# Expert weights subtracted on VectorE alone, x transposed through two PSUM banks, and the last chunk's second tile three units behind the first

## The chip, the cores and the metric

The kernel runs on one core of a Trainium2 chip. The metric is the device time of one execution in microseconds (us). The engines are named as the profile names them: PE is TensorE's matmuls and PEld its weight loads, DVE is VectorE, ACT is ScalarE, POOL is GpSimd, SP is SyncE, which issues most DMAs.

## What is computed

Three layers follow each other. All inputs are float32.

```python
# attention with a threshold: 4 batches, 8 heads, 576 positions, 64 per head
scores = scale * q @ k.T;  keep scores >= max - tau;  softmax;  @ v
x = attn_out.transpose(0, 2, 1, 3).reshape(2304, 512)
# top-1 mixture of 8 experts, D = 512, F = 1024
e_idx = argmax(x @ w_gate)
for e in range(8):
    mask = e_idx == e
    h = maximum(x[mask] @ w1[e], 0)
    out[mask] = gate_w[mask] * eom[mask, e] * (h @ w2[e])
# dense layer, 512 -> 2048 -> 512
h = x @ w_in;  g = maximum(0.01 * h, h);  return g @ w_out
```

## The kernel before

A float32 operand of a matmul is split in two parts that TensorE takes at its faster rate (fp32r): a "hi" part, which a cast makes, and a "lo" part, which is the operand less its hi part. Each product is the sum of three matmuls (`PASSES`): hi by hi, hi by lo, lo by hi. So each block of weights and each block of x needs a cast (L1554 on ACT, L1556 on DVE) and a subtraction (L1559, on DVE or POOL).

The program has an attention stage, an expert stage and a dense stage. In the expert stage there is one window of tokens for each place r = 0 to 7, in order of size (`CAPS` = 400, 368, 324, 320, 296, 272, 248, 216 columns), after a first window of 216. A window's work is:

- eight weight blocks (q = 0 to 7, 128x1024 each) loaded by SP into a ring of four buffers `raw` (`r_raw`), cast (`hi`) and subtracted (`lo`) into a ring of 12 in `arena` (`r_w`). The buffer in `raw` comes free when the subtraction has ended;
- three or four tiles of at most 108 tokens, fetched by a gather that POOL issues (L1627), transposed by TensorE into a PSUM bank (L1636, "xT"), cast (`xh`) and subtracted (`xl`) out of that bank into `arena`. The ring `r_tp` has as many places as transposed tiles may hold a bank;
- the first product, eight groups of 12 matmuls (L1667, "L1"), each into a bank of its own, at most three at a time (`r_l1`); its result goes through a ReLU on ACT (`hh`, L1675) and a subtraction on DVE (`hl`, L1681), which frees the bank;
- the second product, eight groups of 12 matmuls (L1708, "L2") into four banks.

PSUM has eight banks, which all of this shares. Meanwhile DVE also cuts the 64-bit words of the dense layer's weights down to float32 (`narrow`, four operations to a block: L1304, L1310, L1316, L1326).

The dense stage takes chunks of 512 tokens, and a last one of 256 (n = 256, two tiles of 128). A chunk has 16 units f. A unit is 12 matmuls of the first product (L1870, "h2"), then on ACT and DVE the leaky ReLU (`t`, L1877, and `g`, L1881) and the split of g (`gh`, L1554; `gl`, L1559), then for each tile three matmuls of the second product (L1896, "out") into the tile's bank. After the last unit each tile is scaled out of PSUM by ACT (L1919, "oev") and scattered to the result by an indirect DMA that POOL issues (L1925, "st").

No order is written out by hand. `Plan` holds a list of operations, each with its candidate engines and their costs, its dependencies, the rings it takes from (`acq`) and gives back to (`rel`), and a priority, which is a due time. It places them one after the other at the earliest time on an engine, and emits them in order of the planned start; on the chip each engine then runs its own list strictly in that order, and waits where data or a buffer is not there.

Of the kernel before, what the change touches and what calls it, by code (L numbers as in the profile page):

```python
# [8 lines left out]
F32 = mybir.dt.float32  # L9
# [1519 lines left out]
def experts(pl, ctx, tc, st, R, ar, w1, w2, w_in, w_out, xrows, yT, wtab, wf, out):  # L1529

    nc = tc.nc
    ps, bk, ident = st.ps, st.bk, st.ident
# [4 lines left out]
    r_raw, r_w, r_x, r_h, r_sm, r_ys = Ring(len(raw)), Ring(ar.NW), Ring(ar.NX), Ring(ar.NH), Ring(len(sm)), Ring(len(ys))  # L1537
    r_l1, r_tp, r_l2 = Ring(3), Ring(1), Ring(1)
    AD = ("act", "dve")
# [6 lines left out]
    def ev(n, ptr=0.0):  # L1546
        return (0.16 + 0.00083 * n + ptr, 0.14 + 0.00106 * n + ptr)
# [4 lines left out]
    def copy(o, out, in_):  # L1552
        if o.eng == "act":
            nc.scalar.copy(out=out, in_=in_)  # L1554
        else:
            nc.vector.tensor_copy(out=out, in_=in_)  # L1556

    def subtract(o, out, in0, in1):
        (nc.vector if o.eng == "dve" else nc.gpsimd).tensor_tensor(out=out, in0=in0, in1=in1, op=ALU.subtract)  # L1559


    free = st.t_over + 0.1


    wins, t = [(None, PRE, 0.0)], 96 * mm(PRE) + 4
# [8 lines left out]
    for r, n, tw in wins:  # L1574
# [7 lines left out]
        for q in range(4 if r is None else 0, 8):  # L1582
# [13 lines left out]
            if r is None and q < 6:  # L1596
                t = staged(st, q)
# [12 lines left out]
            O["lo", r, q] = pl.add(  # L1610
                *((("dve", "pool"), (1.5, 2.7)) if r is not None else ("dve", 1.4)), lambda o, f=lo, ld=ld, h=a: f(o, ld, h), [a], need - 11.9, rel=[(r_raw, ld)], label="lo", at=free + 3 if r is None else free)

# [212 lines left out]
    chunks = [(c, min(512, NT - c)) for c in range(0, NT, 512)]  # L1825
    r_o, r_g, r_t, r_h2 = Ring(1), Ring(2), Ring(2), Ring(4)
    tgs = [ys_ for ys_ in st.tg]
# [4 lines left out]
    for ci, (c0, n) in enumerate(chunks):  # L1832
# [24 lines left out]
        AHEAD = 8  # L1857
        outs = None
        for f in range(FF // 128):
# [22 lines left out]

            def g_hi(o, tt, n=n):
                copy(o, ar.g(o.slots[r_g][0])[:, 0, 0:n], tgs[tt.slots[r_t][0]][:, 1, 0:n])

            def g_lo(o, tt, gh, n=n):
                t = ar.g(gh.slots[r_g][0])
                subtract(o, t[:, 1, 0:n], tgs[tt.slots[r_t][0]][:, 1, 0:n], t[:, 0, 0:n].bitcast(F32))

            def prod(o, first, gh, f=f, u=u, c2=c2, m=m):  # L1890
                w = V[u, 1].rearrange("p a (c f) -> p a c f", c=2)
                g = ar.g(gh.slots[r_g][0])
                k = 0
                for gi, wi in ((0, 0), (0, 1), (1, 0)):
                    for t in range(m):
                        nc.tensor.matmul(  # L1896
                            out=bank(first, t), lhsT=g[:, gi, 128 * t:128 * t + 128], rhs=w[:, wi, c2, :],
                            start=(f == 0 and k == 0), stop=(f == FF // 128 - 1 and k == 2),
                        )
                    k += 1  # L1900
# [4 lines left out]
            gg = pl.add("dve", ev(n)[1], lambda o, a=a, tt=tt, f=act_g: f(o, a, tt), [tt], bf + 3.1, rel=[(bk, a), (r_h2, a)], label="g")  # L1905
            gh = pl.add(AD, (0.62, 0.4), lambda o, tt=tt, f=g_hi: f(o, tt), [gg], bf + 3.2, acq=[(r_g, 1)], label="gh")
            gl = pl.add("dve", 0.74, lambda o, tt=tt, gh=gh, f=g_lo: f(o, tt, gh), [gh], bf + 3.3, rel=[(r_t, tt)], label="gl")
            last_o = pl.add(
# [5 lines left out]
        for t in range(m):  # L1914
# [8 lines left out]
            def st_o(o, e, t=t, c0=c0):  # L1923
# [5 lines left out]

            e = pl.add(AD, ev(512, 0.1), lambda o, fb=outs, f=oev: f(o, fb), [last_o, e, mts[c0 // 128 + t]], base + CH + t, acq=[(r_sm, 1)],  # L1930
                       rel=[(bk, outs), (r_o, outs)] if t == m - 1 else [], label="oev")
# [132 lines left out]
```

## Time and profile before

| | |
|---|---|
| median of 3 runs | 1006.02 us (1003.82 to 1007.94) |
| the profiled execution | 1004.9 us, of which the span from first to last instruction is 1002.7 us |
| PE busy | 960.8 us, 96% of the span |
| DVE busy | 641.3 us, 64% |
| ACT busy | 507.3 us, 51% |
| POOL busy | 264.4 us, 26% |
| expert stage | about 338 to 595 us of the span |
| dense stage | about 595 us to the end |

A share of busy time over the whole span is a mean over the stages. The granted clock of TensorE is 1.00 at 2.4 GHz and 0.50 at 1.2 GHz.

### The profile page before, as it was taken

What the parts mean: (1) busy time and instruction counts of PE and PEld (TensorE: products, weight loads), DVE (VectorE), ACT (ScalarE), POOL (GpSimd) and SP (SyncE); (2) the same over time, 40 slices, a digit from 0 to 9 for tenths busy, and PEclk for the clock granted to TensorE, in tenths of its full rate; (3) what the DMA queues carried; (4) which work ended last, traced back from release to release, by engine and by line L of the source; (5) the groups of instructions that cost most, each with busy time, mean ns of one, the idle gap of its engine ahead of it and who ended that gap; (6) DMA issues with size and microseconds to landing.
All of it is one profiled execution on the core that took longest, in us unless ns stands there. A gap on an engine that the chain in (4) does not pass through costs nothing. (4 is left out here: it accounts for less than half of the span.)

```text
span 1002.7 us, 16909 instructions
## 1 busy us (share of the span) xinstructions
PE 960.8 (96%) x6118; PEld 844.5 (84%) x6118; DVE 641.3 (64%) x1231; ACT 507.3 (51%) x1009; POOL 264.4 (26%) x325
## 2 busy tenths in 40 slices
PE   6999999999999889999899999999999999999994
PEld 6788888888887789989899998888888888888883
DVE  7888998998996775988986548983223223222331
ACT  7778787888874355454555435443223222322321
POOL 4433333333112444442446402321000100100000
PEclk9999999999999899999999999999999999999998
DMA  5523432431242688589887552422000200100000
GB/s 143 150 71 90 129 72 74 138 81 49 75 152 69 191 222 293 190 303 305 301 286 266 166 178 77 119 70 74 11 1 1 84 1 0 63 1 1 18 25 22
DMA packets 63578, 114.32 MB, mean 114 GB/s; under 512 B 15424, under 2 KB 32832, under 8 KB 62976
## 3 DMA queue, kind: packets, MB, share of 16 engines
q1 hardware_dynamic: 56912, 92.02, 29.4%
q0 software_dynamic: 6576, 21.15, 7.6%
q8 instruction: 50, 0.82, 0.3%
q14 instruction: 40, 0.33, 0.1%
HBM read 84.72 MB, written 19.09 MB: 104 GB/s over the span
## 5 line engine op out<-in xcount | busy, mean ns | idle before, releaser
L1870 PE MATMUL ps<-arena 128*128 128x512 f32 (+1 forms) x960 | 207.6, 368 | 0.0
L1896 PE MATMUL ps<-arena 128*128 128x512 f32 x864 | 206.8, 389 | 0.0
L1870 PEld LDWEIGHTS ps<-arena 128*128 128x128 f32 x960 | 168.7, 188 | 30.9
L1559 DVE TENSOR_TENSOR arena<-raw,arena 128x512 fp32r<-128x512 f32 (+2 forms) x131 | 122.7, 941 | 111.1 <-PE ps L1896 67.0
L1896 PEld LDWEIGHTS ps<-arena 128*128 128x128 f32 x864 | 161.3, 188 | 33.2 <-ACT arena L1554 0.2
L1554 ACT CAST arena<-raw 128x1024 fp32r<-128x1024 f32 (+2 forms) x153 | 121.4, 803 | 107.5 <-PE ps L1896 56.4
L1881 DVE TENSOR_TENSOR raw<-ps,raw 128x512 f32<-128x512 f32 (+1 forms) x80 | 50.6, 636 | 134.3 <-ACT raw L1877 134.2
L1708 PE MATMUL ps<-arena 128*128 128x216 f32 (+7 forms) x864 | 128.9, 307 | 6.4 <-ACT arena L1675 4.7
L1708 PEld LDWEIGHTS ps<-arena 128*128 128x128 f32 x864 | 122.7, 193 | 7.4 <-ACT arena L1675 5.1
L1667 PE MATMUL ps<-arena 128*128 128x400 f32 (+7 forms) x768 | 114.1, 308 | 8.7 <-ACT arena L1554 3.2
L493 DVE SCALAR_TENSOR_TENSOR em<-ps,th,e 128x576 f32<-128x576 f32 x144 | 115.6, 811 | 9.2 <-ACT e L485 8.4
L1877 ACT ACTIVATE raw<-ps 128x512 f32<-128x512 f32 (+1 forms) x80 | 43.9, 553 | 150.9 <-PE ps L1870 150.9
L1667 PEld LDWEIGHTS ps<-arena 128*128 128x128 f32 x768 | 110.9, 190 | 10.3 <-DVE arena L1559 3.7
L474 DVE TENSOR_REDUCE nm<-ps 128x1 f32<-128x576 f32 x144 | 107.3, 752 | 17.0 <-PE ps L465 15.2
L485 ACT ACTIVATE e<-ps,nm 128x576 f32<-128x576 f32 x144 | 105.9, 744 | 6.8 <-DVE nm L474 6.2
L465 PE MATMUL ps<-k,qt 128*128 128x288 f32 x512 | 99.5, 322 | 2.3 <-ACT qt L256 0.9
L1925 POOL DMA_INDIRECT out_dram<-sm,oidx x18 | 17.8, 987 | 302.7 <-ACT sm L1919 269.8
L250 ACT COPY eta<-ps 128x512 f32<-128x512 f32 (+1 forms) x152 | 79.4, 543 | 23.3 <-PE ps L522 19.9
L522 PE MATMUL ps<-ident,em 128*128 128x128 f32 x576 | 84.2, 274 | 2.1 <-DVE em L493 1.3
L465 PEld LDWEIGHTS ps<-k,qt 128*128 128x128 f32 x512 | 74.6, 193 | 8.2 <-DVE em L493 2.5
L1559 POOL TENSOR_TENSOR arena<-raw,arena 128x1024 fp32r<-128x1024 f32 x23 | 58.8, 2562 | 61.7 <-ACT arena L1554 59.9
L601 PE MATMUL ps<-eta,rv 128*64 128x288 f32 x512 | 69.5, 412 | 1.9 <-ACT eta L250 1.9
(221 smaller groups left out, 1087.7 us busy)
## 6 DMA issues: line engine op xcount, KB each, us to landing
raw<-in_moe_w_dram SPq DMA_DIRECT2D x70, 512.0 KB
k<-k POOLq DMA_DIRECT2D x30, 304.0 KB
dw<-in_moe_w_in_dram SPq DMA_DIRECT2D x16, 512.0 KB
dw<-in_moe_w_out_dram SPq DMA_DIRECT2D x16, 512.0 KB
rk<-in_k_dram SPq DMA_DIRECT2D x16, 256.0 KB
rq<-in_q_dram SPq DMA_DIRECT2D x16, 256.0 KB
rv<-in_v_dram SPq DMA_DIRECT2D x16, 256.0 KB
xrows<-xt SPq DMA_DIRECT2D x4, 1024.0 KB
```

Source lines behind the costliest of these rows:

```text
L250: nc.scalar.copy(out=out, in_=in_)
L465: nc.tensor.matmul(out=s[:, c, :], lhsT=lhs, rhs=T[kk, P][:, off + c * HALF:off + (c + 1) * HALF], start=(m == 0), stop=(m == 2 * len(ops) ...
L474: nc.vector.tensor_reduce(out=T["nm", n], in_=T["sc", n], axis=AX.XY, op=ALU.max, negate=True)
L485: nc.scalar.activation(out=T["e", n].rearrange("p (a c) -> p a c", a=2), in_=T["sc", n], func=AF.Exp, bias=T["nm", n][:, 0:1], scale=1.0,)
L493: nc.vector.scalar_tensor_tensor(out=T["em", P, t][:, h, :].rearrange("p (a c) -> p a c", a=2), in0=T["sc", n], scalar=T["th", n][:, 0:1], ...
L522: nc.tensor.transpose(out=bank(o)[:, c * 128:(c + 1) * 128], in_=T["em", P, t][:, h, 64 * h + c * 128:64 * h + (c + 1) * 128], identity=ident,
L1554: nc.scalar.copy(out=out, in_=in_)
L1559: (nc.vector if o.eng == "dve" else nc.gpsimd).tensor_tensor(out=out, in0=in0, in1=in1, op=ALU.subtract)
L1667: nc.tensor.matmul(out=bank(o)[:, 0:n], lhsT=w[:, wi, 128 * f:128 * f + 128], rhs=xx[:, xi, c, :], start=(c == 0 and i == 0), stop=(c == K ...
L1708: nc.tensor.matmul(out=bank(first, d)[:, 0:n], lhsT=w[:, wi, k0:k0 + 128], rhs=hx[:, xi, :], start=(f == 0 and i == 0), stop=(f == 7 and i ...
L1870: nc.tensor.matmul(out=bank(o)[:, 0:n], lhsT=w[:, wi, c, 128 * c2:128 * c2 + 128], rhs=y[:, c, 0:n], start=(k == 0), stop=(k == 3 * KD - 1),)
L1896: nc.tensor.matmul(out=bank(first, t), lhsT=g[:, gi, 128 * t:128 * t + 128], rhs=w[:, wi, c2, :], start=(f == 0 and k == 0), stop=(f == FF ...
```

## The change

Three edits in `experts`. The places of `r_tp` go from one to two. The subtraction of an expert's weights has DVE as its only candidate, planned at 1.25, where it had DVE at 1.5 or POOL at 2.7. In the chunk with two tiles, each unit's products are two operations, one for each tile, and the second tile's has a due time three units later; the split of g there goes to a ring of four half-width buffers (`r_gs`) in the two buffers that `r_g` had, with smaller planned costs, and the first tile is scaled out as soon as its own products are done.

```diff
-    r_l1, r_tp, r_l2 = Ring(3), Ring(1), Ring(1)
+    r_l1, r_tp, r_l2 = Ring(3), Ring(2), Ring(1)
...
             O["lo", r, q] = pl.add(
-                *((("dve", "pool"), (1.5, 2.7)) if r is not None else ("dve", 1.4)), lambda o, f=lo, ld=ld, h=a: f(o, ld, h), [a], need - 11.9, rel=[(r_raw, ld)], label="lo", at=free + 3 if r is None else free)
+                "dve", 1.25 if r is not None else 1.4, lambda o, f=lo, ld=ld, h=a: f(o, ld, h), [a], need - 11.9, rel=[(r_raw, ld)], label="lo", at=free + 3 if r is None else free)
...
-    r_o, r_g, r_t, r_h2 = Ring(1), Ring(2), Ring(2), Ring(4)
+    r_o, r_g, r_t, r_h2, r_gs = Ring(1), Ring(2), Ring(2), Ring(4), Ring(4)
+
+    BEHIND = 3
...
-        outs = None
+        outs, before, tiles = None, last_o, [None] * m
...
+            def g_at(o, n=n):
+                if n > 256:
+                    return ar.g(o.slots[r_g][0])[:, :, 0:n]
+                i = o.slots[r_gs][0]
+                return ar.g(i // 2)[:, :, 256 * (i % 2):256 * (i % 2) + n]
...
-            gh = pl.add(AD, (0.62, 0.4), lambda o, tt=tt, f=g_hi: f(o, tt), [gg], bf + 3.2, acq=[(r_g, 1)], label="gh")
-            gl = pl.add("dve", 0.74, lambda o, tt=tt, gh=gh, f=g_lo: f(o, tt, gh), [gh], bf + 3.3, rel=[(r_t, tt)], label="gl")
+            small = m == 2
+            gh = pl.add(AD, (0.36, 0.3) if small else (0.62, 0.4), lambda o, tt=tt, f=g_hi: f(o, tt), [gg, before if small else None], bf + 3.2,
+                        acq=[(r_gs if small else r_g, 1)], label="gh")
+            gl = pl.add("dve", 0.45 if small else 0.74, lambda o, tt=tt, gh=gh, f=g_lo: f(o, tt, gh), [gh], bf + 3.3, rel=[(r_t, tt)], label="gl")
+            if small:
+                for t in range(2):
+                    o = pl.add(
+                        "pe", 3 * 0.228, lambda o, gh=gh, f=prod, fb=outs, t=t: f(o, fb or o, gh, ts=(t,)), [gl, *wo, tiles[t], outs],
+                        bf + 5.4 + 5.4 * BEHIND * t, acq=[(bk, 2), (r_o, 1)] if outs is None else [], rel=[(r_gs, gh)] if t else [], label="out")
+                    outs = outs or o
+                    tiles[t] = last_o = o
+                continue
...
-            e = pl.add(AD, ev(512, 0.1), lambda o, fb=outs, f=oev: f(o, fb), [last_o, e, mts[c0 // 128 + t]], base + CH + t, acq=[(r_sm, 1)],
+            e = pl.add(AD, ev(512, 0.1), lambda o, fb=outs, f=oev: f(o, fb), [tiles[t] or last_o, e, mts[c0 // 128 + t]], base + CH + t, acq=[(r_sm, 1)],
```

The planner turns these into other orders on each engine from the expert stage on. TensorE's list at the start of the expert stage, where L1708 with 216 columns is the first window's second product, L1636 are the transposes of x and L1667 with 400 columns is the first product of the window r = 0. Before:

```order
L1708 MATMUL ps<-arena 128x216 x12
L1636 MATMUL ps<-ident,sm_70 128x108 x4
L1708 MATMUL ps<-arena 128x216 x36
L1636 MATMUL ps<-ident,sm_71 128x108 x4
L1708 MATMUL ps<-arena 128x216 x36
L1636 MATMUL ps<-ident,sm_72 128x108 x4
L1708 MATMUL ps<-arena 128x216 x12
L1636 MATMUL ps<-ident,sm_73 128x76 x4
L1667 MATMUL ps<-arena 128x400 x96
```

The same place of the change:

```order
L1708 MATMUL ps<-arena 128x216 x12
L1636 MATMUL ps<-ident,sm_70 128x108 x4
L1708 MATMUL ps<-arena 128x216 x12
L1636 MATMUL ps<-ident,sm_71 128x108 x4
L1708 MATMUL ps<-arena 128x216 x24
L1636 MATMUL ps<-ident,sm_72 128x108 x4
L1636 MATMUL ps<-ident,sm_73 128x76 x4
L1708 MATMUL ps<-arena 128x216 x48
L1636 MATMUL ps<-ident,sm_70 128x108 x4
L1636 MATMUL ps<-ident,sm_71 128x108 x4
L1667 MATMUL ps<-arena 128x400 x96
```

The last tile of r = 0 (128x76) stood right ahead of L1667 and now stands 48 matmuls ahead of it, and the first two tiles of r = 1 have come in between. TensorE's list two windows on, where L1708 with 368 columns is the second product of r = 1 and L1667 with 324 columns the first product of r = 2, as a difference:

```order
 L1667 MATMUL ps<-arena 128x368 x96
 L1708 MATMUL ps<-arena 128x368 x12
 L1636 MATMUL ps<-ident,sm_70 128x108 x4
-L1708 MATMUL ps<-arena 128x368 x36
+L1708 MATMUL ps<-arena 128x368 x12
 L1636 MATMUL ps<-ident,sm_71 128x108 x4
-L1708 MATMUL ps<-arena 128x368 x24
+L1708 MATMUL ps<-arena 128x368 x12
 L1636 MATMUL ps<-ident,sm_72 128x108 x4
-L1708 MATMUL ps<-arena 128x368 x24
+L1708 MATMUL ps<-arena 128x368 x60
 L1667 MATMUL ps<-arena 128x324 x96
```

The last transpose stood 24 matmuls ahead of L1667 and now stands 60 ahead. TensorE's last rows, where L1870 (L1872 in the changed file) is h2 and L1896 (L1904) is out; before, and then of the change:

```order
L1870 MATMUL ps<-arena 128x256 x12
L1896 MATMUL ps<-arena 128x512 x6
L1870 MATMUL ps<-arena 128x256 x12
L1896 MATMUL ps<-arena 128x512 x18
L2059 UNCONDITIONAL_BRANCH
```

```order
L1872 MATMUL ps<-arena 128x256 x12
L1904 MATMUL ps<-arena 128x512 x6
L1872 MATMUL ps<-arena 128x256 x12
L1904 MATMUL ps<-arena 128x512 x27
L2077 UNCONDITIONAL_BRANCH
```

Nine products more stand behind the last h2. By the PSUM banks that the built program writes, the 27 alternate between the tiles in groups of three, second tile first, until the first tile has its last group, and the nine at the very end are all the second tile's; before, every group of six served both tiles.

## Rows read from the trace of the kernel before

**Rows 1.** The page, its first part: busy time, share of the span, instructions

```profile
PE 960.8 (96%) x6118; PEld 844.5 (84%) x6118; DVE 641.3 (64%) x1231; ACT 507.3 (51%) x1009; POOL 264.4 (26%) x325
```

**Rows 2.** Busy time by stretch: stretch, length, PE, PEld, DVE, ACT, POOL, clock, DMA share, GB/s

```profile
380.00:600.00 220.00, 212.55 (x1548) 209.20 (x1547) 164.21 (x222) 106.98 (x185) 90.81 (x57) 1.00 0.76 253
410.00:530.00 120.00, 114.07 (x806) 112.41 (x805) 107.53 (x133) 62.66 (x104) 51.21 (x28) 1.00 0.84 284
354.80:358.00 3.20, 0.49 (x2) 0.23 (x2) 3.03 (x9) 2.54 (x5) 2.82 (x2) 1.00 0.87 278
358.00:364.00 6.00, 6.00 (x25) 5.95 (x26) 5.64 (x6) 2.24 (x5) 2.49 (x2) 0.72 1.00 322
595.00:988.90 393.90, 393.89 (x1829) 329.45 (x1828) 160.81 (x240) 126.33 (x226) 37.52 (x31) 1.00 0.12 39
```

**Rows 3.** Waits in 330 to 600 us: us in total, times, longest

```profile
ACT arena L1554 <- DMA raw<-in_moe_w_dram: 19.4, 12, 5.3
```

**Rows 4.** Timeline of PE, expert stage: start, us, instruction, [idle before <-releaser]

```profile
356.21 0.45 PE L1667 MATMUL ps<-arena 128*128 128x400 f32 x1 [1.44 <-ACT arena L1554]
357.96 4.32 PE L1667 MATMUL ps<-arena 128*128 128x400 f32 x15 [1.29 <-DVE arena L1559]
...
431.34 0.41 PE L1667 MATMUL ps<-arena 128*128 128x324 f32 x1 [1.73 <-ACT arena L1554]
432.22 4.99 PE L1667 MATMUL ps<-arena 128*128 128x324 f32 x32 [0.46 <-DVE arena L1559]
...
492.42 3.40 PE L1667 MATMUL ps<-arena 128*128 128x296 f32 x23 [1.17 <-DVE arena L1559]
...
499.81 6.87 PE L1667 MATMUL ps<-arena 128*128 128x296 f32 x48 [1.75 <-DVE arena L1681]
...
528.44 1.78 PE L1667 MATMUL ps<-arena 128*128 128x272 f32 x12 [0.81 <-DVE arena L1681]
```

**Rows 5.** Groups by form, DVE and POOL, 380 to 600 us: busy us, mean ns

```profile
L1559 DVE TENSOR_TENSOR arena<-raw,arena 128x1024 fp32r<-128x1024 f32 x41 | 53.6, 1322 | 22.3 <-ACT arena L1554 18.7 <-issue 2.7 <-PE ps L1667 0.6
L1304 DVE TENSOR_SCALAR cv<-dw 128x512 int32<-128x512 int32 x18 | 22.5, 1252 | 4.5 <-DMA dw<-in_moe_w_out_dram 4.2 <-DMA dw<-in_moe_w_in_dram 0.3
L1326 DVE SCALAR_TENSOR_TENSOR cv<-dw,cv 128x512 f32<-128x512 f32 x18 | 19.7, 1095 | 2.6 <-ACT dw L1322 1.9
...
L1559 POOL TENSOR_TENSOR arena<-raw,arena 128x1024 fp32r<-128x1024 f32 x18 | 45.9, 2554 | 45.6 <-ACT arena L1554 45.5
```

**Rows 6.** Timeline, DVE operations apart from a subtraction on POOL and beside one

```profile
411.33 0.67 DVE L1326 SCALAR_TENSOR_TENSOR cv<-dw,cv 128x512 f32<-128x512 f32 x1
412.38 0.41 DVE L1304 TENSOR_SCALAR cv<-dw 128x512 int32<-128x512 int32 x1
414.93 1.21 DVE L1559 TENSOR_TENSOR arena<-raw,arena 128x1024 fp32r<-128x1024 f32 x1
...
460.00 2.75 POOL L1559 TENSOR_TENSOR arena<-raw,arena 128x1024 fp32r<-128x1024 f32 x1 [4.00 <-ACT arena L1554]
460.60 2.71 DVE L1326 SCALAR_TENSOR_TENSOR cv<-dw,cv 128x512 f32<-128x512 f32 x1
```

**Rows 7.** Timeline, one unit of the last chunk: gh on ACT, h2 on PE, gl on DVE

```profile
974.53 0.41 ACT L1554 CAST arena<-raw 128x256 fp32r<-128x256 f32 x1 [0.55 <-DVE raw L1881]
974.73 1.60 PE L1870 MATMUL ps<-arena 128*128 128x256 f32 x12
975.00 0.43 DVE L1559 TENSOR_TENSOR arena<-raw,arena 128x256 fp32r<-128x256 f32 x1 [0.56 <-ACT arena L1554]
```

**Rows 8.** Timeline, the end of the program

```profile
984.62 4.27 PE L1896 MATMUL ps<-arena 128*128 128x512 f32 x18
...
988.70 1.26 ACT L1919 ACTIVATE sm<-ps,mt 128x512 f32<-128x512 f32 x2 [2.48 <-PE ps L1896]
989.66 0.98 POOL L1925 DMA_INDIRECT out_dram<-sm,oidx  x1 [31.12 <-ACT sm L1919]
993.16 0.98 POOL L1925 DMA_INDIRECT out_dram<-sm,oidx  x1 [2.51 <-DMA out_dram<-sm,oidx]
```

More of the change, by code (lines that the diff above doesn't have):

```diff
@@ L1881, in act_g, with g_hi, g_lo, prod @@
                 nc.vector.tensor_tensor(out=t[:, 1, 0:n], in0=bank(a)[:, 0:n], in1=t[:, 0, 0:n], op=ALU.max)
[L1883 to L1890, printed above, removed]
+            def g_at(o, n=n):
[3 more added lines that the diff above has]
+                return ar.g(i // 2)[:, :, 256 * (i % 2):256 * (i % 2) + n]
+            def g_hi(o, tt, n=n, at=g_at):
+                copy(o, at(o)[:, 0], tgs[tt.slots[r_t][0]][:, 1, 0:n])
+            def g_lo(o, tt, gh, n=n, at=g_at):
+                t = at(gh)
+                subtract(o, t[:, 1], tgs[tt.slots[r_t][0]][:, 1, 0:n], t[:, 0].bitcast(F32))
+            def prod(o, first, gh, f=f, u=u, c2=c2, ts=range(m), at=g_at):
                 w = V[u, 1].rearrange("p a (c f) -> p a c f", c=2)
-                g = ar.g(gh.slots[r_g][0])
+                g = at(gh)
                 k = 0
                 for gi, wi in ((0, 0), (0, 1), (1, 0)):
-                    for t in range(m):
+                    for t in ts:
                         nc.tensor.matmul(
```

## The prediction

> **What bounds the kernel now.** I read the page first: TensorE is busy 960.8 of 1002.7 us [rows 1], so a change can only win where TensorE waits, or after its last matmul. Then the busy time by stretch: from 595 to 988.9 us TensorE is busy 393.89 of 393.90 us [rows 2], so in the dense stage nothing is to be had before its last matmul. From 380 to 600 us it is busy 212.55 of 220 us, and from 354.8 to 358 us only 0.49 of 3.2 us [rows 2]. Next, TensorE's own timeline, which has each wait with what ended it [rows 4]. At the head of three windows L1667 waits for x, first for its cast on ACT and then for its subtraction on DVE: 1.44 and 1.29 us (r = 0), 1.73 and 0.46 us (r = 2), 1.17 us (r = 4); together 6.1 us. Two more waits, 1.75 and 0.81 us, are for L1681, the `hl` on DVE that frees a bank of the first product; together 2.6 us.  Last, the end of the program: TensorE ends at 984.62 + 4.27 = 988.89 us, ACT scales both tiles out from 988.70 on, the first store starts at 989.66 us, and the second, long ready, at 993.16 us, after a wait of 2.51 us for the first one's data to land [rows 8]. So the end is TensorE's last matmul plus two stores in a row.
>
> **The tail.** The number of matmuls stays: 18 products stood behind the last h2, now 27, because nine fewer stood ahead of it. What moves is the first tile's end. A product costs 4.27 / 18 = 0.237 us [rows 8]. Nine products of the second tile alone stand at the end, so the first tile is complete 9 x 0.237 = 2.1 us earlier, is scaled out 2.1 us earlier, and its store starts at 987.5 us in place of 989.66. The second tile is scaled out when it was, and would be ready for its store at 989.66 us; it waits for the first store, which sets the pace, 993.16 - 989.66 = 3.5 us after its start: 991.0 us. **Minus 2.1 us.** It can't be more while the stores follow each other, and it is 0 if the first tile doesn't end early.
> What could cost something here is the ring of four: the cast gh of a unit now waits for the second tile's product four units back, and by the order that product stands just ahead of an h2 of 12 matmuls, behind which the unit's own first product comes. gh and gl take 0.41 and 0.43 us with about 0.06 us between them, 0.9 us from 974.53 to 975.43, against an h2 of 1.60 us that hides them [rows 7]. I take 0. If it were short by 0.3 us in each of the eleven units that stand so, it would be 3.3 us.
>
> **The transposes.** No transpose is added or taken away; each stands earlier on TensorE. At r = 0 the last tile of x stood directly ahead of L1667, so its cast and subtraction lay bare. Now 48 matmuls of 216 columns stand between, and two transposes of the next window. The rows show no wait of this form with that much work between; the nearest bound is the 1.44 + 1.29 us that are there with none. I take both waits as gone: minus 2.7 us. The transposes that have come ahead of L1667 wait in turn for gathers, and these for indices that DVE makes; before, two subtractions on POOL stood ahead of those gathers, and they are gone. Were the gathers late, the wait would be here again, up to the same 2.7 us.
> The clock adds to it. In 354.8 to 358 us TensorE nearly stood still, and from 358 to 364 us the granted clock is 0.72 [rows 2], a mixture of 2.4 and 1.2 GHz. That costs 6 x (1 - 0.72) = 1.7 us of work. At the other waits, none over 1.75 us, the clock stays at 1.00 over the stretch as a whole [rows 2, 4]. Without the wait there is nothing that lowers it: minus 1.7 us.
> Of this the Trainium skill says, in "TensorE: Matmul & The Clock Gate", section "What's actually happening", that the slow clock is the default, that activity releases it, and that the number of slow matmuls differs between runs of one kernel. By that the 1.7 us need not be in every timed run, and without them the forecast would be 996.5 us in place of 994.8. The trace has it in its one execution, and I keep it.
> At r = 2 the last transpose moves from 24 to 60 matmuls ahead of L1667, at r = 4 likewise far ahead: minus 2.2 and minus 1.2 us, 0 if x is late for another reason.
>
> **The subtractions.** 18 of them leave POOL between 380 and 600 us, at 2.55 us, and come to DVE [rows 5], where one takes 1.21 us [rows 6]: 18 x 1.21 = 22 us more for DVE. But DVE gets time back. L1326 takes 0.67 us, and 2.71 us where it started 0.60 us after a subtraction on POOL and ended 0.56 us after it; L1304 is 0.41 us when alone [rows 6], and its mean is 1.252 us [rows 5]. Against the times when alone, the excess is (1.252 - 0.41) x 18 = 15.2 us for L1304, (1.095 - 0.67) x 18 = 7.7 us for L1326 and (1.322 - 1.21) x 41 = 4.6 us for L1559: 27.5 us. If all of it comes from POOL, DVE is 5 us less busy than its 164.21 of 220 us [rows 2], though it does more. Where a subtraction moves, its buffer in `raw` also comes free after 1.2 us in place of 2.6, so the loads start earlier.
> That makes the two waits for `hl` shorter, because DVE comes to L1681 earlier; but more subtractions now stand ahead of it in the one queue. Between 0 and 2.6 us I take half: minus 1.3 us.
> The Trainium skill, "SBUF — State Buffer", section "Who interferes with whom", says that a VectorE instruction with two SBUF inputs and a GpSimd instruction that reads SBUF exclude each other for the whole instruction, so that the second one waits for the first to end. By this rule every such delay ends with POOL's subtractions, both waits would go in full, and the forecast would be 993.5 us; by the rows it is 994.8. The trace agrees in the pair at 460 us: DVE's L1326 ran on to 463.31, POOL's ended at 462.75.
>
> **Sum.** 2.1 + 2.7 + 1.7 + 2.2 + 1.2 + 1.3 = 11.2 us off the profiled execution's 1004.9 us (2.2 us over its span) is 993.7. The median of the runs stands 1.1 us above that execution, so the forecast is 994.8, said as **995 us**.
>
> **Rivals.**
> A. The waits for x go only at the start, where the order shows it clearest; at r = 2 and r = 4, and for `hl`, as much comes back elsewhere, because DVE is busy 107.53 of 120 us from 410 to 530 us [rows 2] and one queue now holds all. Then 2.1 + 2.7 + 1.7 = 6.5 us off the median: 999.5 us. For it speaks that DVE share, against it that part of it is waiting for POOL.
> B. The planner's new order opens as many waits in the expert stage as it closes, and only the tail is left: 1004 us. Against it speaks that x waits had a plain cause, a tile of x too close to its use.
> C. The two banks do nothing: three banks for the first product, four for the second and two for x are nine, and PSUM has eight, so the second is often not to be had. With the subtractions neutral and the tail hidden, 1006 us. Against it: the order already has the transposes earlier, wherever the bank comes from.
> D. Slower: DVE runs in order, and each weight block's subtraction waits there for a cast, which waits for its load. ACT waits 19.4 us, 12 times, for weights from memory [rows 3]; a subtraction on POOL waited without holding up `hl`, now every one of them does. If TensorE gets all of that and keeps the gains, it is 19.4 - 11.2 = 8.2 us slower: 1014 us. It decides from 11.2 of the 19.4 us on. Against it: no wait of TensorE in the rows is for weights. If DVE's excess had nothing to do with POOL, this would start sooner: by the length of the stretch, 18 x 120 / 220 = 10 of the subtractions fall in 410 to 530 us, 12 us, and DVE has 12.5 us idle there [rows 2].
>
> **How the numbers follow.** The forecast has 0.62, A 0.17, B 0.11, C 0.03, D 0.07. The runs of before spread over 4.1 us, so about 0.5%, or 5 us, is what the measurement can tell from no change. Faster than 1001 us are the forecast and most of A: 0.76; within 0.5% are the rest of A, B and C: 0.17; slower is D: 0.07. The forecast's own range is 992 to 998: all waits gone would be 12.5 us off, 993.5, and the runs spread by 2 us each way. The range that holds 8 in 10 goes from 991, all of it and a fast run, to 1003, which takes in A and reaches towards B.
>
> **What would show it.** In the changed profile L1667 of r = 0 starts without a wait, and the granted clock after it is 1.00; no wait for x at r = 2 and r = 4; L1304 has a mean near 0.42 us and L1326 near 0.68 over the expert stage, and DVE is busy under 164 us there; the second store starts 3.5 us after the first as before, but 2.1 us after TensorE's last matmul in place of 4.3. The prediction is wrong if TensorE waits for gathers ahead of L1636, if the waits for L1681 grow, or if TensorE pauses between the units of the last chunk.

## The result, and the profile after

| | before | after |
|---|---|---|
| median, compared on one chip | 1004.92 us (1001.35 to 1007.94, 4 runs) | 993.35 us (992.94 to 994.29, 4 runs) |
| the profiled execution, its span | 1004.9, 1002.7 us | 992.94, 991.2 us |
| PE, DVE, POOL busy | [rows 1] | 956.7, 630.0, 208.1 us |
| last matmul's end to the start of the last store | 4.27 us [rows 8] | 2.46 us |

The ratio is 0.9886, with an interval of 0.9861 to 0.9912: 1.1% faster. The forecast was 995 us. Lines after the change: h2 is L1872, t L1879, g L1883, out L1904, oev L1937, st L1943; the others keep their numbers.

Busy time by stretch of the changed kernel, with the columns of [rows 2]:

```profile
380.00:600.00 220.00, 220.00 (x1586) 216.57 (x1585) 162.54 (x249) 116.64 (x195) 46.72 (x39) 1.00 0.76 257
410.00:530.00 120.00, 120.00 (x865) 119.56 (x864) 100.20 (x155) 68.11 (x114) 19.96 (x18) 1.00 0.88 305
354.80:358.00 3.20, 0.00 (x0) 0.00 (x0) 0.69 (x1) 1.04 (x1) 2.56 (x2) 0.96 0.94 296
358.00:364.00 6.00, 5.96 (x27) 5.95 (x28) 4.00 (x9) 1.92 (x4) 1.00 (x1) 0.74 1.00 362
585.80:979.20 393.40, 393.40 (x1826) 329.12 (x1824) 161.17 (x241) 127.00 (x225) 38.71 (x32) 1.00 0.12 37
```

From 380 us to the last matmul TensorE no longer waits at all: 220.00 of 220.00 us, where it was 212.55. But the third and fourth lines are hardly better than before: ahead of r = 0 TensorE still stands still, and its clock behind that is still a mixture, 0.74. TensorE's timeline there:

```profile
353.50 0.54 PE L1636 MATMUL ps<-ident,sm 108*128 108x108 f32 x4
358.04 0.98 PE L1636 MATMUL ps<-ident,sm 108*128 108x108 f32 x4 [4.00 <-DMA sm<-xrows,gidx]
358.70 18.85 PE L1667 MATMUL ps<-arena 128*128 128x400 f32 x96
```

The wait for x is gone, as forecast; in its place the second transpose of r = 1 waits 4.00 us for its gather. DVE and POOL from 380 to 600 us, by form, as in [rows 5]:

```profile
L1559 DVE TENSOR_TENSOR arena<-raw,arena 128x1024 fp32r<-128x1024 f32 x60 | 72.5, 1220 | 30.2 <-ACT arena L1554 28.9 <-PE ps L1667 0.6 <-DMA yT<-ys 0.5
...
L1559 POOL TENSOR_TENSOR arena<-raw,arena 128x1024 fp32r<-128x1024 f32 x1 | 2.4, 2398 | 22.6 <-ACT arena L1554 22.6
```

DVE does 60 subtractions of this form in place of 41, and yet is busy 162.54 us in place of 164.21: L1304 has a mean of 420 ns (was 1252) and L1326 of 685 (was 1095). The end of the program, timeline:

```profile
972.90 6.31 PE L1904 MATMUL ps<-arena 128*128 128x512 f32 x27
...
977.21 0.69 ACT L1937 ACTIVATE sm<-ps,mt 128x512 f32<-128x512 f32 x1 [1.86 <-PE ps L1904]
979.25 0.69 ACT L1937 ACTIVATE sm<-ps,mt 128x512 f32<-128x512 f32 x1 [1.35 <-PE ps L1904]
...
978.17 0.98 POOL L1943 DMA_INDIRECT out_dram<-sm,oidx  x1 [29.18 <-ACT sm L1937]
981.67 0.98 POOL L1943 DMA_INDIRECT out_dram<-sm,oidx  x1 [2.51 <-DMA out_dram<-sm,oidx]
```

ACT scales the first tile 2.04 us before the second, and the last store starts at 981.67, 2.46 us after the last matmul ends (972.90 + 6.31 = 979.21).

**Where the 11.5 us of span came from.** Ahead of the first L1708 the new execution is 0.8 us earlier (338.28 for 339.05), where nothing was changed. From there to the dense stage (595.38 before, 585.79 after) it gains 8.8 us, the dense stage gives 0.1, the tail 1.8. Of the 8.8, waits that are gone make 7.4: 2.19 (r = 2), 1.17 (r = 4), 2.56 (`hl`), and 1.52 of short "issue" waits. The wait at r = 0 grew, 4.00 for 2.73 us, which takes 1.3 back. The remaining 2.7 us lie in the work itself. From the start of L1667 of r = 0 to that of r = 1 it is 37.06 us, where before it was 38.60 without its wait of 1.29 us; two transposes went from this interval, to stand ahead of it. In windows whose waits went, the same interval, net of its waits, shrank by 0.2 to 0.5 us each. In the two that had no waits, r = 3 and r = 7, it stayed as it was (29.24 and 29.23 us, 21.42 and 21.43). All this compares one execution with one.

### The profile page after: what moved, and what is told of

It is laid out like the page before. It is cut to its first block, busy times and chain, and to the rows that moved or that the text cites. A ratio compares the mean times of both kernels' runs of the same rounds, so it can differ in the third digit from the quotient of the medians.

```text
span 991.2 us, 16887 instructions
## 1 busy us (share of the span) xinstructions
PE 956.7 (97%) x6118; PEld 842.2 (85%) x6118; DVE 630.0 (64%) x1255; ACT 510.1 (51%) x1007; POOL 208.1 (21%) x303
## 5 line engine op out<-in xcount | busy, mean ns | idle before, releaser
L1559 DVE TENSOR_TENSOR arena<-raw,arena 128x1024 fp32r<-128x1024 f32 (+2 forms) x153 | 142.3, 936 | 109.4 <-PE ps L1904 58.1
L1872 PE MATMUL ps<-arena 128*128 128x512 f32 (+1 forms) x960 | 207.8, 368 | 0.0
L1904 PE MATMUL ps<-arena 128*128 128x512 f32 x864 | 206.9, 389 | 0.0
L1872 PEld LDWEIGHTS ps<-arena 128*128 128x128 f32 x960 | 168.8, 188 | 30.9
L1904 PEld LDWEIGHTS ps<-arena 128*128 128x128 f32 x864 | 161.4, 188 | 32.9
L1883 DVE TENSOR_TENSOR raw<-ps,raw 128x512 f32<-128x512 f32 (+1 forms) x80 | 50.7, 636 | 144.5 <-ACT raw L1879 144.5
L1708 PE MATMUL ps<-arena 128*128 128x216 f32 (+7 forms) x864 | 127.4, 306 | 4.7 <-ACT arena L1675 4.6
L1708 PEld LDWEIGHTS ps<-arena 128*128 128x128 f32 x864 | 122.2, 192 | 5.5 <-ACT arena L1675 5.0
L1879 ACT ACTIVATE raw<-ps 128x512 f32<-128x512 f32 (+1 forms) x80 | 44.2, 555 | 160.2 <-PE ps L1872 160.1
L1667 PE MATMUL ps<-arena 128*128 128x400 f32 (+7 forms) x768 | 112.4, 306 | 0.0
L1667 PEld LDWEIGHTS ps<-arena 128*128 128x128 f32 x768 | 110.5, 190 | 0.0
L1943 POOL DMA_INDIRECT out_dram<-sm,oidx x18 | 17.9, 995 | 302.0 <-ACT sm L1937 269.0
L522 PEld LDWEIGHTS ps<-ident,em 128*128 128x128 f32 x576 | 67.6, 141 | 4.5 <-DVE em L493 1.7
```

Of the source, the lines that this page charges most:

```text
L522: nc.tensor.transpose(out=bank(o)[:, c * 128:(c + 1) * 128], in_=T["em", P, t][:, h, 64 * h + c * 128:64 * h + (c + 1) * 128], identity=ident,
L1667: nc.tensor.matmul(out=bank(o)[:, 0:n], lhsT=w[:, wi, 128 * f:128 * f + 128], rhs=xx[:, xi, c, :], start=(c == 0 and i == 0), stop=(c == K ...
L1708: nc.tensor.matmul(out=bank(first, d)[:, 0:n], lhsT=w[:, wi, k0:k0 + 128], rhs=hx[:, xi, :], start=(f == 0 and i == 0), stop=(f == 7 and i ...
L1872: nc.tensor.matmul(out=bank(o)[:, 0:n], lhsT=w[:, wi, c, 128 * c2:128 * c2 + 128], rhs=y[:, c, 0:n], start=(k == 0), stop=(k == 3 * KD - 1),)
L1904: nc.tensor.matmul(out=bank(first, t), lhsT=g[:, gi, 128 * t:128 * t + 128], rhs=w[:, wi, c2, :], start=(f == 0 and k == 0), stop=(f == FF ...
```

## The experiments

The theory after the result: the gain outside the tail comes from the subtractions leaving POOL, since DVE's operations then run at their own length; the second bank gives little, since a late gather took the place of the wait that it removed. The rival is the prediction's own account: the second bank removes the waits for x (7.8 of 11.2 us with the clock), the subtractions are worth 1.3. e1 to e4, e5 to e8 and e9 to e12 each ran on one chip beside the kernel before.

### One part undone: e1, e2, e3

e1 puts the last chunk's code back as before (the whole last part of the change); e2 and e3 change one line each:

```diff
-    r_l1, r_tp, r_l2 = Ring(3), Ring(2), Ring(1)
+    r_l1, r_tp, r_l2 = Ring(3), Ring(1), Ring(1)
```

```diff
-                "dve", 1.25 if r is not None else 1.4, lambda o, f=lo, ld=ld, h=a: f(o, ld, h), [a], need - 11.9, rel=[(r_raw, ld)], label="lo", at=free + 3 if r is None else free)
+                *((("dve", "pool"), (1.5, 2.7)) if r is not None else ("dve", 1.4)), lambda o, f=lo, ld=ld, h=a: f(o, ld, h), [a], need - 11.9, rel=[(r_raw, ld)], label="lo", at=free + 3 if r is None else free)
```

> The changed kernel with the last chunk as before: both tiles' products together, one ring for g. Theory: the stores in a row set the end, so the second store starts 4.3 us after TensorE's last matmul in place of the 2.5 us of the changed kernel, and the time is about 1.8 to 2.1 us longer, 995.3 us by the 993.35 of the changed kernel. Rival: the products in groups of three cost TensorE something between the units; then the stretch from the first h2 of the last chunk to the last product is shorter here than in the changed kernel, and the time is less than 1 us longer.

> The changed kernel with one place in the ring of transposes, so that TensorE's order at the start of the expert stage is that of before; subtractions on DVE alone. Theory: x close to its use is what cost the waits, so L1667 waits again for cast and subtraction of x at r = 0, about 2.5 us with 1.7 us of slow clock behind it; the wait of 4.0 us for a gather is gone. At r = 2 the order has the last transpose 48 matmuls ahead of L1667 (24 before), so no wait there. About 0 to 2 us shorter or longer than the changed kernel, 991 to 996 us. Rival: the two banks as such give the gain; then waits for x stand at r = 0, r = 2 and r = 4 as before, and the time is 6 us longer, 999 us.

> The changed kernel with weights subtracted on DVE or POOL as the planner chooses, as before. Theory (a subtraction on POOL stops DVE's operations for as long): L1304 has a mean over 1 us in the expert stage again, as against 0.42, and TensorE waits for L1681 about 2.6 us and more; 996 to 999 us. Rival (the two banks alone made the waits go): DVE's means rise too, but TensorE waits for nothing from r = 1 on, and the time is within 1 us of the changed kernel.

e1 took 999.88 us (996.37 to 1005.82, 12 runs), 0.9901 of before (0.9865 to 0.9937); e2 1000.66 (995.98 to 1006.02, 6 runs), 0.9899 (0.984 to 0.9959); e3 1007.87 (1002.03 to 1010.68, 12 runs), 0.997 (0.9935 to 1.0005). All three times lie above what was expected (995.3, 991 to 996, 996 to 999 us). On this chip the kernel before lies higher too, at 1010.13 us (1003.63 to 1018.58), so the ratios and the rows say more than the times. In e1 the last store starts 4.27 us after the last matmul, as before:

```profile
979.32 4.27 PE L1896 MATMUL ps<-arena 128*128 128x512 f32 x18
...
987.86 0.98 POOL L1925 DMA_INDIRECT out_dram<-sm,oidx  x1 [2.52 <-DMA out_dram<-sm,oidx]
```

So the tail is worth 4.27 - 2.46 = 1.8 us. TensorE's waits of e2 from 330 to 600 us (what waited <- for what, total, times, longest):

```profile
PE ps L1708 <- issue: 4.8, 11, 1.1
PE ps L1667 <- DVE arena L1559: 2.0, 1, 2.0
PE ps L1667 <- ACT arena L1554: 0.7, 1, 0.7
```

With one bank the wait for x comes back at r = 0 alone, 2.7 us. Those at r = 2 and r = 4, which the prediction laid to the second bank, stay away. But in e2 the planner also puts the last transpose further ahead of L1667 than before (48 matmuls for 24 at r = 2, 60 for 48 at r = 4), so e2 alone doesn't part DVE's speed from this order. (The "issue" waits are taken up below.) In e3, with two banks, TensorE waits 5.1 us in four pieces for L1681, twice the 2.6 of before. L1304 has a mean of 885 ns there, not over 1 us as expected, and L1310, the next in DVE's list, 1192 ns, against 420 and 684 in the changed kernel. That speaks for the subtractions.

### One part alone: e9, e10, e11

The same three edits, each made alone in the kernel before.

> The kernel before with one part of the change alone: the weight subtractions of the expert layers stand on VectorE. Theory (most of the gain comes from this part): L1304 averages 0.42 us between 380 and 600 us, the waits of TensorE for x at r=2 and r=4 and for L1681 are gone, the wait at r=0 stays (2 to 3 us), and the time is 5 to 8 us below the kernel before. Rival (the second bank removes the waits for x, as the prediction put it): the waits at r=2 (1.73 + 0.46) and r=4 (1.17) stay, only those for L1681 go, and the time is 1 to 3 us below the kernel before.

> The kernel before with one part of the change alone: x is transposed through two banks, the subtractions stay where they were. Theory (the second bank alone matters little): waits for x or for a gather of 2 to 5 us around 355 us, the waits for L1681 stay at 2 us or more, and the time is within 3 us of the kernel before. Rival (the prediction's: the second bank removes 6.1 us of waits for x and the slow clock): no waits for x, time 5 to 8 us below the kernel before.

> The kernel before with one part of the change alone: the second tile of the last chunk stands three units behind the first. Theory: the last store starts 2.4 to 2.5 us after TensorE's last matmul in place of 4.3, the expert layers are as before, and the time is 1.5 to 2.5 us below the kernel before. Rival (the ring of four or the second store's wait gives it back): TensorE pauses between the units of the last chunk, or the last store stands 4 us or more behind the last matmul, time as before.

| | time | ratio to before | TensorE's waits from 340 to 600 us, without "issue" |
|---|---|---|---|
| e9, subtractions alone | 997.64 us (995.66 to 1004.62, 4 runs) | 0.9892 (0.983 to 0.9954) | x at r = 0, 2.7 us; no other |
| e10, two banks alone | 1011.68 us (1005.62 to 1013.41, 10 runs) | 1.0019 (0.9987 to 1.0051) | gather 3.6; L1681 5.5 in 4 |
| e11, tail alone | 1007.59 us (1003.9 to 1013.31, 10 runs) | 0.9975 (0.9941 to 1.0009) | x at r = 0, 2, 4, and 0.6 us at r = 6; L1681 3.0 in 3 |

The timelines of TensorE, those rows of e9 and then of e10 that begin with a wait for data behind the first L1708:

```profile
356.67 0.45 PE L1667 MATMUL ps<-arena 128*128 128x400 f32 x1 [0.74 <-ACT arena L1554]
359.12 19.13 PE L1667 MATMUL ps<-arena 128*128 128x400 f32 x95 [1.99 <-DVE arena L1559]
```

```profile
358.19 0.66 PE L1636 MATMUL ps<-ident,sm 108*128 108x108 f32 x4 [3.59 <-DMA sm<-xrows,gidx]
437.90 7.39 PE L1667 MATMUL ps<-arena 128*128 128x324 f32 x48 [0.93 <-DVE arena L1681]
468.47 7.30 PE L1667 MATMUL ps<-arena 128*128 128x320 f32 x48 [0.74 <-DVE arena L1681]
499.20 9.60 PE L1667 MATMUL ps<-arena 128*128 128x296 f32 x48 [2.75 <-DVE arena L1681]
530.84 7.83 PE L1667 MATMUL ps<-arena 128*128 128x272 f32 x60 [1.06 <-DVE arena L1681]
```

This decides for the theory and against the rival. The ratios of all runs fall into two groups: with the subtractions on DVE they are 0.9886 to 0.9901 (the changed kernel, e1, e2, e9), and with the subtractions as before 0.997 to 1.0019 (e3, e10, e11), whatever the bank and the tail are. From its first L1708 behind the wait for L1675 to its last matmul e9 takes 641.2 us (340.21 to 981.41), the kernel before 649.8 (339.05 to 988.89), the changed kernel 640.9 (338.28 to 979.21). So in these executions the subtractions alone give 8.6 of the 8.9 us. Of the 8.6, waits for x and for L1681 make 5.9, and 1.2 are "issue" waits (1.5 us before, 0.3 in e9), whose cause is open. By the medians e9 is 10.1 us below the kernel before, more than the 5 to 8 expected.

The second bank alone does remove the waits for x at r = 2 and r = 4, but as much comes back as waits for L1681. The longest of these costs more than itself. Behind its 2.75 us the granted clock is 0.50, which is 1.2 GHz, and the 48 matmuls take 9.60 us; before, behind a wait of 1.75 us, it stayed at 1.00 and they took 6.87 [rows 4]. With the columns of [rows 2], e10 and then the kernel before:

```profile
499.20:505.20 6.00, 6.00 (x24) 6.00 (x25) 5.02 (x10) 1.98 (x6) 0.00 (x0) 0.50 1.05 387
...
499.80:505.80 6.00, 5.99 (x43) 6.00 (x44) 3.82 (x10) 1.91 (x5) 0.00 (x0) 1.00 1.02 376
```

Both kinds of wait are one delay, DVE being late, seen at two places, and the kernel before shows where the waits for x come from. At r = 4 its last transpose already had 48 matmuls, 7.27 us, between it and L1667, which still waited 1.17 us for x. TensorE's rows, then POOL's, then DVE's:

```profile
483.60 0.44 PE L1636 MATMUL ps<-ident,sm 80*128 80x80 f32 x4
483.84 7.27 PE L1708 MATMUL ps<-arena 128*128 128x320 f32 x48
...
487.31 2.92 POOL L1559 TENSOR_TENSOR arena<-raw,arena 128x1024 fp32r<-128x1024 f32 x1 [1.32 <-ACT arena L1554]
...
487.88 2.63 DVE L1304 TENSOR_SCALAR cv<-dw 128x512 int32<-128x512 int32 x1
491.88 0.48 DVE L1559 TENSOR_TENSOR arena<-ps,arena 128x320 fp32r<-128x320 f32 x1
```

The cast of x had ended on ACT at 487.54. DVE's subtraction of x stood behind L1304, which took 2.63 us beside POOL's subtraction in place of 0.41, and two more operations. At r = 2 the same L1304 takes 2.12 us. In the plan L1310 follows it, L1322 on ACT follows L1310 (429.43 to 430.12), and behind L1322 stands the cast that L1667 waited for; POOL, DVE and ACT:

```profile
425.99 3.12 POOL L1559 TENSOR_TENSOR arena<-raw,arena 128x1024 fp32r<-128x1024 f32 x1 [2.98 <-ACT arena L1554]
...
427.27 2.12 DVE L1304 TENSOR_SCALAR cv<-dw 128x512 int32<-128x512 int32 x1
...
430.21 0.68 ACT L1322 ACTIVATE dw<-dw 128x512 f32<-128x512 f32 x1 [4.31 <-issue]
430.78 0.51 ACT L1554 CAST arena<-ps 128x432 fp32r<-128x432 f32 x1
```

So the bank moves the delay, and the subtractions end it. What DVE's speed would do at the old distances is not shown: in e9, as in e2, the last transpose of r = 2 and r = 4 also stands further ahead.

In e11 the last store starts 2.47 us after the last matmul (996.08 for 987.30 + 6.31). The gain of 1.8 us is there in the rows, and too small for these times: the medians differ by 0.2 us.

### More on POOL, with TensorE's order kept: e5

Every second subtraction (odd q) goes to POOL. TensorE's list of instructions is that of the changed kernel.

```diff
-                "dve", 1.25 if r is not None else 1.4, lambda o, f=lo, ld=ld, h=a: f(o, ld, h), [a], need - 11.9, rel=[(r_raw, ld)], label="lo", at=free + 3 if r is None else free)
+                *(("pool", 2.7) if r is not None and q % 2 else ("dve", 1.25 if r is not None else 1.4)), lambda o, f=lo, ld=ld, h=a: f(o, ld, h), [a], need - 11.9, rel=[(r_raw, ld)], label="lo", at=free + 3 if r is None else free)
```

> TensorE's order is that of the changed kernel; every second weight subtraction of the expert layers is put back on GpSimd. Theory (a subtraction on GpSimd holds up the operations that VectorE runs beside it): the unpacking operations of VectorE's first group of four (L1304, 0.42 us each in the changed kernel) average 0.7 us or more between 380 and 600 us, TensorE waits again for the second halves of hidden units (L1667 <- DVE L1681) by 1 to 5 us in all, and the time is 3 to 12 us above the changed kernel. Rival (VectorE has room for everything, only the order counts; GpSimd's part costs nothing): L1304 stays at 0.42 us, no such waits, time within 3 us of the changed kernel.

1008.83 us (1005.84 to 1010.48, 6 runs), 1.0046 of before (1.0023 to 1.0069): slower than the kernel before, and 15.5 us above the changed kernel's 993.35, measured on another chip, where 3 to 12 were expected. L1304 averages 872 ns, L1326 1123, and the 31 subtractions left on DVE 1776 ns, where they are 1220 in the changed kernel. TensorE waits 5.8 us for L1681 and 7.0 us for gathers (4.0 in the changed kernel), which now stand behind subtractions in POOL's queue. One of the waits for L1681 in the rows, POOL's timeline first, then DVE's, then TensorE's:

```profile
471.90 3.05 POOL L1559 TENSOR_TENSOR arena<-raw,arena 128x1024 fp32r<-128x1024 f32 x1 [0.24 <-ACT arena L1554]
...
473.36 1.86 DVE L1304 TENSOR_SCALAR cv<-dw 128x512 int32<-128x512 int32 x1 [0.63 <-DMA dw<-in_moe_w_in_dram]
475.15 0.48 DVE L1681 SCALAR_TENSOR_TENSOR arena<-ps,arena 128x320 fp32r<-128x320 f32 x1
...
475.68 8.85 PE L1667 MATMUL ps<-arena 128*128 128x320 f32 x48 [2.56 <-DVE arena L1681]
```

L1304, 0.42 us alone, starts beside POOL's subtraction and ends at 475.22, 0.27 us after it (474.95). L1681 stands behind it, and TensorE, out of banks, waits 2.56 us for L1681. The 48 matmuls behind the wait take 8.85 us, with a granted clock of 0.61 from 475.6 to 480 us; the 48 ahead of it took 7.20, at 1.00.

### The late gather: e4 and e7

e4 lets the transposes of r = 1 come only after the first product of r = 0. e7 leaves them and makes the token numbers (L1081 to L1086, from which the gathers of r = 1 on are issued) earlier on DVE. In e7's plan one transpose of r = 0 also comes ahead of the first L1708.

```diff
-            b = pl.add("pe", 0.45, lambda o, f=xt, g=g: f(o, g), [g], lead, acq=[(bk, 1), (r_tp, 1)], rel=[(r_sm, g)], label="xT")
+            b = pl.add("pe", 0.45, lambda o, f=xt, g=g: f(o, g), [g], lead, after=[O["L1", 1]] if r == 1 else [], acq=[(bk, 1), (r_tp, 1)], rel=[(r_sm, g)], label="xT")
```

```diff
-    others = pl.add("dve", 1.2, R.others, [], -13, at=free + 7, label="tb")
+    others = pl.add("dve", 1.2, R.others, [], -13, at=free + 0, label="tb")
```

> The changed kernel with the transposes of r = 1 kept behind the first product of r = 0, so that no transpose stands directly ahead of that product. Theory: the wait of 4.0 us is the gather's own lateness, and nothing else is late there; it goes, the slow clock behind it (1.5 us) too, and the time is 5 us shorter, 988 us. Rival: weights of r = 0 land late too (ACT waited for one of them until 355.7 us), and L1667 waits for them instead; then a wait of 1 to 3 us stands at L1667 with releaser ACT or DVE, the clock falls all the same, and the time is 0 to 3 us shorter.

> The changed kernel with the table of token numbers for the later experts (L1081 to L1086) worked out on VectorE at the start of the expert layers, some 10 us earlier, so that the gathers of r=1 start earlier. Theory (the 4.0 us that TensorE waits ahead of L1667 of r=0 is the late gather and nothing else, and the slow clock behind it comes of that wait): the wait for sm is gone or under 0.5 us, the first 96 products of L1667 last 17.8 us as against 18.85, and the time is 4 to 6 us below the changed kernel, 987 to 990. Rival (another wait stands right behind it, for the copies of x or for the weights of the first product): a wait of 1 to 4 us at the same place with another releaser, time within 2 us of the changed kernel.

e4 took 991.36 us (989.31 to 1006.16, 8 runs), 0.9811 of before (0.976 to 0.9861). In its profiled execution, one of 1006.16 us with 5.4 us of "issue" waits, the first product of r = 0 starts without a wait at 355.60 and lasts 17.81 us, at a granted clock of 1.00; a wait for x of 1.69 + 0.96 us stands at r = 1. So the gather's wait and its slow clock went, as its theory had it, but the time is above the 988 expected. e7 took 988.79 us (987.37 to 990.51, 4 runs), 0.9861 of before (0.9845 to 0.9877). Its timeline of TensorE around r = 0, and DVE's row that ends the token numbers:

```profile
353.51 0.90 PE L1636 MATMUL ps<-ident,sm 108*128 108x108 f32 x8
354.18 17.73 PE L1667 MATMUL ps<-arena 128*128 128x400 f32 x96
...
339.05 0.18 DVE L1086 TENSOR_SCALAR gidx<-tk 128x28 int32<-128x28 f32 x1
```

In the changed kernel this row stands at 348.51, the second gather behind it was issued at 350.73, and the gathers of this stretch took 6.9 us (median) from issue to landing, with the DMA engines busy to 0.94 (the stretch from 354.8 to 358 us above). So the data came at about 358 us. With the numbers 9.5 us earlier the wait is gone, the clock is 1.00 from 354.8 to 364 us, and the 96 matmuls take 17.73 us in place of 18.85. The last matmul ends at 973.58 in place of 979.21: 4.5 us from an earlier start of r = 0, 1.1 from the clock. Ahead of the first L1708 TensorE now waits 3.73 us for a gather (at 337.32) where it waited 4.62 us for L1675, and L1708 starts at 338.45 in place of 338.28, so nothing is won or lost there. e7 is 0.5% below the changed kernel's 993.35, measured on another chip; on e7's own chip e6 and e8, below, differ by e7's edit alone, 994.05 and 988.72 us.

### The second bank once the gather is early: e12

e7 with `Ring(1)` for `r_tp`.

> The changed kernel with early token numbers (988.8 us) and only one bank for the transposes. Theory (the second bank is worth the wait for x at r=0 and its slow clock, once the gather isn't late): a wait for x of 2 to 3 us ahead of L1667 of r=0 and 3 to 5 us more than with two banks, 991.5 to 994. Rival (with early gathers the second bank brings nothing): no such wait, time within 1.5 us of 988.8.

989.03 us (988.4 to 995.32, 4 runs), 0.9808 of before (0.9752 to 0.9865): no worse than e7's 988.79 on another chip, so the theory was wrong here and the rival right. The timeline of TensorE shows why:

```profile
352.46 0.43 PE L1636 MATMUL ps<-ident,sm 76*128 76x76 f32 x4
352.69 1.58 PE L1708 MATMUL ps<-arena 128*128 128x216 f32 x12
354.11 0.54 PE L1636 MATMUL ps<-ident,sm 108*128 108x108 f32 x4
354.42 3.90 PE L1667 MATMUL ps<-arena 128*128 128x400 f32 x20
```

In e9 L1667 stood directly behind the last transpose of r = 0, which ended at 355.94, and could run on only at 359.12, 3.2 us later. Here it ends at 352.89, and 1.5 us of other work between is enough: with all transposes of r = 0 3 to 5.5 us earlier, DVE and ACT are done with x sooner as well. DVE's last subtraction of x ends at 353.85 and six small operations (L1098 to L1102) come behind it; in e9 they stood ahead of it, and it ended at 359.07. With the subtractions on DVE and the numbers early, one bank is enough.

### The small gathers: e6 and e8

In the profiles of e2, e3, e4, e10 and e11, and of the kernel before, TensorE shows 1.5 to 5.4 us of short "issue" waits between 534 and 568 us, where POOL issues 18 gathers of 4 bytes a row (L1818); e1 and e9 show 0.7 and 0.3 us. e6 moves these into the dense stage, e8 does this and e7's edit.

```diff
-        mts.append(pl.add("pool", 1.1, weight, [oi, last, pool_last], t2 + 2 * j, dma=0.3, label="mt"))
+        mts.append(pl.add("pool", 1.1, weight, [oi, last, pool_last], t2 + 2 * j, dma=0.3, label="mt", at=t2 + 25.0))
```

> The changed kernel with its 18 small gathers of table weights (L1818, 4 bytes for each of 128 rows) moved from the end of the expert layers into the dense layer. Theory (these gathers are what makes TensorE stand still in short issue waits between 530 and 570 us in some executions): no issue waits of TensorE over 0.5 us in all between 520 and 600 us, the executions lie closer together, with few above 996, and the fast ones stay at 991 to 994. Rival (the issue waits belong to the place in the program or to the chip, not to the gathers): executions of 1000 to 1006 us are as frequent as in the earlier runs, or the issue waits turn up where the gathers now stand.

> Both of the last two together: token numbers early and small gathers late. Theory: their gains add, 987 to 990 us, and the executions lie within some 4 us of each other. Rival: no more than the better of the two, or the spread remains.

e6 took 994.05 us (993.09 to 994.72, 4 runs), 0.9906 of before (0.9889 to 0.9922); e8 988.72 us (988.53 to 988.95, 4 runs), 0.9855 (0.9839 to 0.9872), the same as e7: the late small gathers add nothing to it. Neither shows issue waits in that stretch. But e7, which ran beside them with the gathers where they were, shows none either, and so does the changed kernel. The gathers alone don't bring the waits about; whether they are needed for them stays open.

## Why the prediction was right, and where it was not

The time was right, 993.35 us for 995, and the sum nearly so: 11.5 us off the span, 11.2 forecast. But two terms were wrong and made up for each other, and that they did was luck: the 4.4 us entered for r = 0 and its clock became a loss of 1.3, and what filled the gap stood in no term, 1.3 us more for `hl`, 2.7 in the work between the waits, 1.5 of issue waits and 0.8 ahead of the first L1708.

- **The transposes** failed, at the step "I take both waits as gone: minus 2.7 us", and with it "minus 1.7 us" for the clock. The wait for x went, and the wait for the gather stood in its place, 4.00 us, with the clock at 0.74. The prediction had named this place ("Were the gathers late, the wait would be here again"), and by its own sign ("The prediction is wrong if TensorE waits for gathers ahead of L1636") it was wrong here; but it left this out of the sum, though what decides it could have been read: how long the gathers take from issue to landing, and when DVE has the token numbers. e7 shows that the wait was the gather's lateness, and that the clock fell because of it: with the gather early both are gone, and the 96 matmuls are 1.1 us shorter.
- **r = 2 and r = 4:** both waits went, minus 2.2 and 1.2 us as forecast, but the bank was not needed for it: e2 loses them with one. With two banks and POOL as before, e10 exchanges them for 5.5 us of waits for L1681 in place of 2.6. The cause, a tile of x too close to its use, was read from too few rows. The prediction says "The rows show no wait of this form with that much work between" of 48 matmuls of 216 columns; the trace of before has one at r = 4, 1.17 us with 48 matmuls of 320 columns between.
- **The subtractions** were mis-sized. "Between 0 and 2.6 us I take half" was all of 2.6, and that was the smaller part: e9 makes them worth 8.6 us in all, 3.4 of which the prediction had entered under the bank, and 1.2 of which are issue waits that may not be theirs. The working behind it, DVE's excess from POOL's subtractions, was right in each row: 0.42 us for L1304 and 0.685 for L1326 against "near 0.42" and "near 0.68". DVE's busy time fell 1.7 us, not 5, with 249 instructions in those 220 us in place of 222, and stayed below 164. The slip was to ask only which named waits would end. A late DVE also cost in the work around them (0.2 to 0.5 us in each window), in x waits, and in e10 and e5 in the clock. e5 shows the mechanism with TensorE's order kept. The Trainium skill, "SBUF — State Buffer", section "Who interferes with whom", says that a VectorE instruction with two SBUF inputs contends with a GpSimd instruction that reads SBUF. By that rule the prediction had both waits go in full; the trace agrees, they did. L1304 has one input, so that sentence does not cover it; that it waits for POOL too is shown by its rows at 473.36 in e5 and 487.88 before.
- **The tail** measured 1.8 us for 2.1, with the stores 3.50 us apart as forecast. The count of nine products was one too many: before, the last product of each unit was the second tile's, so the first tile was done one product early, and ACT began with it 0.19 us ahead of TensorE's end [rows 8]. Now ACT begins 2.00 us ahead (977.21 for 979.21). The difference is 1.81, eight products of 0.23. The ring of four cost nothing: the dense stage is busy 393.40 of 393.40 us.
- **Rival D** had the right row and the wrong consequence. ACT's waits for weights rose from 19.4 us [rows 3] to 34.7 (19 times), and TensorE waited for none of it. **Rival C** came close for one part, though not for its reason, the number of banks: by e12 the second bank is worth nothing once the gathers are early. **Rival A** counted on DVE being full from 410 to 530 us; with more to do it is busy 100.20 us there, where it was 107.53.

Open: what brings the issue waits about, what the subtractions alone would do to the waits for x at the old distances, and why the stretch ahead of the first L1708 was 0.8 us shorter. The other start times of L1708 lie at 338.05 to 340.57, so 0.8 us may be no more than the spread from one execution to the next.

## What to carry to other kernels

When VectorE is late, the waits it causes turn up under many names (x, a bank, a copy). Ask which of its instructions run longer than alone, and beside what, before crediting each wait to the edit that stands nearest to it. Moving an instruction earlier on one engine only pays if what feeds it is early too: read how long its DMA takes to land and when its index is made.

## What the runs showed of the hardware beyond this

- From 380 to 600 us DVE with 19 more subtractions of 1.22 us was less busy than without them (162.54 us for 164.21). On POOL one takes 2.4 to 2.6 us in the mean, and with 29 of them there (e5) the program is slower than with 18 (before).
- A small operation can lose as much as a large one. Before the change L1081, which makes the token numbers, took 2.76 us where it ran beside POOL's subtractions; after it 0.57 us, in these timelines of DVE:

```profile
345.65 2.76 DVE L1081 TENSOR_TENSOR scr<-one,tsa 128x224 f32<-128x224 f32 x1
```

```profile
347.48 0.57 DVE L1081 TENSOR_TENSOR scr<-one,tsa 128x224 f32<-128x224 f32 x1
```

- The two indirect stores into the result start 3.49 to 3.51 us apart before, after, and in e1, e6, e7, e9, e10, e11 and e12, whether the second tile is ready with the first or 2 us later.
